# Loading the TensorE-turned part of x ahead of the transposing loads, and copying the padded weights on ScalarE

## The chip, the cores and the metric

One NeuronCore of a Trainium2 chip runs the whole kernel. The metric is device time in microseconds (us) for one execution. The figures of the kernel before are eight timed executions, and one more that the hardware profiler recorded.

## The reference, cut to what matters

```python
x = A_x                                   # 1 x 2048 x 512, bfloat16
g = sigmoid((x * gate_w).sum(-1, keepdims=True))
# A: attention with 32 heads of 16
q, k, v = split_heads(x @ wqkv)
a = softmax(q @ k.T / 4) @ v @ wo
# B: gated feed-forward, hidden width 1792
b = (silu(x @ w_gate) * (x @ w_up)) @ w_down
return g * a + (1 - g) * b
```

The input x enters every product. The attention's exponentials (32 heads, 2048 x 2048 scores each) are most of the work.

## The kernel before, in words

TensorE contracts over partitions, so the products with the weights need x turned: `xT` (line 176) holds x with its 512 columns as four chunks `dc` of 128 partitions, and the 2048 rows along the free axis. The attention works in units of one block of 512 queries and four heads; each unit runs over 16 tiles of 128 keys. For each tile TensorE makes scores (`s_t`, two heads to a tile of 1024 columns), ScalarE takes their exponential (`e_t`), and TensorE multiplies that into `o_ps`. VectorE takes a share of the tiles (`d_t` and `y_t`) by integer arithmetic. Projections, the feed-forward part and the output products are cut in pieces, and a planner with modelled times and due dates (class `Pacer`, lines 48 to 76, and the loop from line 1390) puts these pieces between the score tiles. What comes out is a fixed order of instructions on each engine: `mm`, `act`, `vec` and `queue` (lines 157 to 173) pin that order on TensorE, ScalarE, VectorE and the SyncE (SP) queue.

Before the planner begins there is a prologue, and the change lies wholly in it:

- **Loads.** SP issues six transposing DMAs (line 182), each 1024 rows by 128 columns. For the first half of the rows (0 to 1023) only chunks 0 and 1 come that way; for the second half all four do. I number them T1 to T6 in the order of issue. SP then issues the rest of the value weights (line 194) and of the query and key weights (line 196). ScalarE's queue issues, in this order, 64 columns of the key weights and of the query weights (`wqk`, line 186), the plain load `x_rows` (line 189: rows 0 to 1023, columns 256 to 511, 512 KB, parked in the first part of `wd_t`), and 64 columns of the value weights (line 192).
- **Memsets and padded weights.** VectorE clears small tiles, and twice (lines 239 to 243) sets a group of `kaug` to ones and then copies 64 columns of weights from `wqk` into the spaced layout `wpad`, the key weights first (i = 1), then the query weights (i = 0). `wpad` lies in `mt`.
- **Keeping TensorE busy.** `keep_warm(11)` at line 1026 runs eleven products of a cleared tile into a scratch bank, `warm`.
- **Turning on TensorE.** `turn` (line 1021) multiplies the eight 128 x 128 blocks of a chunk of `x_rows` by an identity: chunk 3 first, which ScalarE copies from `tp` to `xT` (line 1029), then chunk 2, which VectorE copies (line 1033).
- **The first keys and queries.** Lines 1036 to 1043 accumulate `kp0` (1024 keys, two products for each chunk) and `qp0` (512 queries, one product) over the chunks in the order 0, 2, 3, 1, with one more `keep_warm(1)` before the first chunk and between chunks. Chunks 0 and 1 come from T1 and T2, chunks 2 and 3 from `turn`. After that a maximum of the keys (`largest`), a bound, the first values (`v0`), and the first score tile follow, each waiting for the one before.

The planner's first side work is `k0_pieces(2)` and `k0_pieces(3)` (line 1070): keys of the second half, which need T3 to T6. Value pieces (`v_pieces`, line 491) then need the value weights of line 194.

Of the kernel before, what the change touches and what calls it, by code (L numbers as in the profile page):

```python
# [8 lines left out]
ACT = mybir.ActivationFunctionType  # L9
# [70 lines left out]
def kernel(  # L80
# [12 lines left out]
    nc = tc.nc  # L93
    P = 128
    x = A_x.flatten_outer_dims()
    S, D = x.shape
    F = B_w_gate.shape[1]
    DH = 16
# [6 lines left out]
    QBW = 512  # L105
# [40 lines left out]
    def ordered(ins):  # L146
        i = ins.ins
        if i.engine in last_of:
            tc.add_manual_dep(
                i, last_of[i.engine].name,  # L150
                mybir.DependencyInfo(mybir.DependencyClass.NoSync, mybir.DependencyReason.DATA),
                reason="order",
            )
        last_of[i.engine] = i
        return ins

    def mm(*args, **kw):
        return ordered(nc.tensor.matmul(*args, **kw))  # L158

    def act(*args, **kw):  # L160
        ordered(nc.scalar.activation(*args, **kw))  # L161
# [11 lines left out]
    queue = Ordered(nc.sync)  # L173
# [3 lines left out]
    wd_t = big.tile([P, FC, D], BF16, name="wd_t")  # L177
    HALF = DC // 2
    x_rows = wd_t[:, 0:4, :].rearrange("p f d -> p (f d)").rearrange("p (i d) -> p i d", d=HALF * P)
    for t0 in (0, 2 * QBW):  # L180
        for dc in range(DC if t0 else HALF):
            queue.dma_start_transpose(out=xT[:, dc, t0:t0 + 2 * QBW], in_=x[t0:t0 + 2 * QBW, dc * P:(dc + 1) * P])
    wqk = big.tile([P, DC, 2 * D], BF16, name="wqk")
    for c0 in (D, 0):

        nc.scalar.dma_start(out=wqk[:, :, c0:c0 + 64],
                            in_=A_wqkv[:, c0:c0 + 64].rearrange("(dc p) c -> p dc c", p=P))

    nc.scalar.dma_start(out=x_rows, in_=x[0:2 * QBW, HALF * P:D].rearrange("(i p) d -> p i d", p=P))
    rb = big.tile([P, NB, QBW], BF16, name="rb")  # L190
    wv = rb[:, :, :]
    nc.scalar.dma_start(out=wv[:, :, 0:64], in_=A_wqkv[:, 2 * D:2 * D + 64].rearrange("(dc p) c -> p dc c", p=P))
# [2 lines left out]
    for c0 in (D, 0):  # L195
        queue.dma_start(out=wqk[:, :, c0 + 64:c0 + D],
                          in_=A_wqkv[:, c0 + 64:c0 + D].rearrange("(dc p) c -> p dc c", p=P))
# [22 lines left out]
    wpad = [mt[:, i, :].rearrange("p (dc c) -> p dc c", c=P) for i in range(2)]  # L220
# [15 lines left out]
    def ones_rows(engine, g):  # L236

        engine.memset(kaug[:, g, :].bitcast(F32), 1.0019378662109375)
    for i in (1, 0):
        ones_rows(nc.vector, 2 - i)  # L240
        nc.vector.tensor_copy(
            out=wpad[i][:, :, :].rearrange("p dc (j c) -> p dc j c", c=32)[:, :, :, 1:1 + DH],
            in_=wqk[:, :, i * D:i * D + 64].rearrange("p dc (j c) -> p dc j c", c=DH))
    ident = const.tile([P, P], BF16, name="ident")
    nc.gpsimd.memset(ident[:], 1.0)
    nc.gpsimd.affine_select(out=ident[:], in_=ident[:], pattern=[[-1, P]], compare_op=ALU.is_equal,
# [13 lines left out]
    for h in range(8):  # L260
        c = 2 * (h % 4) + h // 4
# [410 lines left out]
    def down_pieces(qb, tq):  # L672

        def end(p):
            t, n = tq, qb * TQ + tq
            share = omg if qb < QB - 1 else ge
            vec.tensor_scalar(out=bblk[:, t, :], in0=p[:, 0:D], scalar1=share[:, n:n + 1],
                              scalar2=None, op0=ALU.mult)
            if qb == QB - 1:
                scaled.add(t)  # L680
            m_free(p, plan.dve)
        return columns(FC, "dps", lambda fc: mt[:, fc, tq * P:(tq + 1) * P], lambda fc: wd_t[:, fc, :],
                       lambda p: later(0.65, lambda: end(p)))
# [314 lines left out]
    def keep_warm(n):  # L998
        for _ in range(n):
            mm(warm[:, :], lhsT=idle[:, 0:P], rhs=idle[:, :], start=True, stop=True)  # L1000
# [22 lines left out]
            mm(ps[k // TQ][:, k % TQ * P:(k % TQ + 1) * P], lhsT=x_rows[:, k, (dc - HALF) * P:(dc - HALF + 1) * P],  # L1023
               rhs=ident[:, :], start=True, stop=True)

    keep_warm(11)
    tp = ps_s.tile([P, 2 * QBW], F32, tag="s", name="tp")
    turn(DC - 1, [tp[:, 0:QBW], tp[:, QBW:2 * QBW]])
    act(out=xT[:, DC - 1, 0:2 * QBW], in_=tp[:, :], func=ACT.Copy)
# [97 lines left out]
    for qb in range(1, QB):  # L1127
        d = qb * KT
# [5 lines left out]
    for qb in range(QB):  # L1134
        for b in range(NB):
            d = UNIT.index((qb, max(2 * b, 1))) * KT
# [30 lines left out]
    for qb in range(QB):  # L1167
# [18 lines left out]
        for tq in range(TQ):  # L1186
            c = pace.add(down_pieces(qb, tq), 0 if qb else 100, a0 + per * (0.6 + 0.3 * (tq + 1) / TQ if qb < QB - 1 else 0.68 + 0.32 * (tq + 1) / TQ), (gus if tq == 0 else prev) + fin_prev + gates)
# [116 lines left out]
    def side(most):  # L1304

        due = any(not c.out() for n in range(plan.slot, plan.slot + 12) for c in need.get(n, []))
        cur = pace.cur
        begun = cur is not None and not cur.out() and cur.i and pace.credit > -3
        c = pick() if pace.credit > 0 or due or begun else None
        if c is None:  # L1310
            return None
        mms, _, takes = c.pieces[c.i][:3]
        mode, two = c.pieces[c.i][3:] or ("C", None)
        if two and two["seq"] == plan.seq:
            return None
        t = m_ready(int(takes)) if takes else 0.0
        if t is None or t > plan.pe or 0.226 * mms + (0.1 if plan.mode != mode else 0.0) > most:
            return None
        return c
# [70 lines left out]
    while au < UNITS:  # L1390
# [10 lines left out]
        if room > 0.02:  # L1401
# [6 lines left out]
            c = side(room + SLACK)  # L1408
# [29 lines left out]
    while closed < UNITS or vops or added or vcur:  # L1438
# [9 lines left out]
        c = side(2.0)  # L1448
# [78 lines left out]
```

## Time and profile before

| | before |
|---|---|
| median of 8 timed executions | 836.04 us (833.89 to 836.71) |
| the profiled execution's own time | 833.6 us |
| span of the profile, first to last instruction | 831.9 us |
| PE (TensorE) busy | 787.5 us (95%), 8117 instructions |
| DVE (VectorE) busy | 796.8 us (96%), 1177 instructions |
| ACT (ScalarE) busy | 810.0 us (97%), 909 instructions |
| POOL (GpSimd) busy | 102.6 us (12%), 124 instructions |
| first exponential of a score tile begins | 17.70 us |
| last score matmul begins | 821.22 us |

The span is the stretch between the first and the last instruction; the execution's own time is 1.7 us more. In the timeline a row has its start, its busy time, the engine, the source line, the operation, the tile written and the tiles read, and in brackets how long the engine stood idle before it and what released it. "ACTq" and "SPq" are those engines' issue of a DMA, not the transfer. In the table by stretches each row has the stretch, its length, the busy time of PE, PEld (weight loads), DVE, ACT and POOL with the number of instructions, the granted TensorE clock as a share of full speed, the busy share of the DMA engines, and GB/s.

### The profile page before, as it was taken

The numbers are of one execution on the slowest core, as the hardware profiler recorded it, in microseconds if no ns is written. First come the engines' busy times: TensorE is split into PE (matmuls) and PEld (weight loads), VectorE is DVE, ScalarE is ACT, GpSimd is POOL, SyncE is SP. The second block draws the span as 40 slices with busy tenths as digits, with TensorE's granted clock in tenths as the row PEclk, the third lists the DMA queues.
The fourth block names the chain that finished last, engine by engine and source line by source line (L and its number), as shares of the span: only waits on it lengthen the run. The fifth ranks groups of instructions, "written<-read, shape, count | busy, mean of one in ns | idle before, by whom it ended". The sixth has DMA issues, their size and how long they took to land.

```text
span 831.9 us, 20393 instructions
## 1 busy us (share of the span) xinstructions
PE 787.5 (95%) x8117; PEld 234.1 (28%) x8118; DVE 796.8 (96%) x1177; ACT 810.0 (97%) x909; POOL 102.6 (12%) x124
## 2 busy tenths in 40 slices
PE   7999999999999999999999999999998989999996
PEld 3322232322222222222222222222222222222222
DVE  5899999999999999999999999999999999999994
ACT  3999999999999999999999999999999999999996
POOL 5010111010101100101111110111111101111100
PEclk9999999999999999999999999999999999999999
DMA  8024347565454345564344464544425455453323
GB/s 177 2 52 97 67 81 138 110 155 100 105 116 84 76 96 112 106 130 88 81 84 87 90 137 88 123 88 100 80 59 115 91 115 107 102 100 72 75 61 76
DMA packets 100647, 79.54 MB, mean 96 GB/s; under 512 B 75696, under 2 KB 88584, under 8 KB 100552
## 3 DMA queue, kind: packets, MB, share of 16 engines
q0 software_dynamic: 12960, 47.19, 29.9%
q1 hardware_dynamic: 84680, 30.07, 15.4%
q10 hardware_dynamic: 2912, 0.98, 0.6%
q8 instruction: 63, 1.03, 0.5%
q14 instruction: 32, 0.26, 0.1%
HBM read 21.36 MB, written 2.34 MB: 28 GB/s over the span
## 4 chain that ended last, share of the span: by engine, by line
PE 38%; ACT 35%; DVE 16%; issue 8%; DMA 2%; SPq 0%; ACTq 0%; DVEq 0%
ACT e_t L161 33%; PE s_t L158 13%; PE o_ps L158 7%; DVE y_t L170 6%; PE gu L158 5%; PE d_t L158 4%; DVE kaug L170 3%; PE dps L158 3%; DVE u_t L170 2%; ACT th L161 2%; PE kp L158 2%; DVE mt L170 2%; PE qp L158 1%; DVE z_t L170 1%; PE vp L158 1%
## 5 line engine op out<-in xcount | busy, mean ns | idle before, releaser
L161 ACT ACTIVATE e_t<-s_t 128x1024 bf16<-128x1024 f32 x844 | 788.1, 1108 | 1.7 <-PE s_t L158 1.2
L158 PE MATMUL s_t<-qx,kaug 64*128 64x512 bf16 x1336 | 273.4, 383 | 25.5 <-ACT e_t L161 22.1
L170 DVE TENSOR_SCALAR y_t<-d_t 128x512 uint16<-128x512 f32 x360 | 234.1, 680 | 1.3 <-PE d_t L158 1.1
L158 PEld LDWEIGHTS <-kaug 64*128 64x128 bf16 x2048 | 112.6, 93 | 341.2 <-issue 332.1
L158 PE MATMUL o_ps<-e_t,vaug 128*32 128x512 bf16 x1688 | 168.1, 390 | 0.3 <-DVE osb L170 0.3
L158 PE MATMUL d_t<-qx,kaug 64*128 64x512 bf16 x296 | 102.1, 380 | 1.4 <-DVE y_t L170 0.6
L791 POOL DMA_DIRECT2D y_t<-u_t x45 | 44.5, 989 | 361.0 <-PE s_t L158 167.4
L158 PEld LDWEIGHTS <-vaug 128*32 128x32 bf16 (+1 forms) x2060 | 50.6, 93 | 120.8 <-issue 119.8
L158 PE MATMUL gu<-xT,wg 128*32 128x512 bf16 x896 | 76.8, 383 | 0.3 <-DMA wg<-in_B_w_gate_dram 0.3
L158 PE MATMUL dps<-wd_t,mt 128*32 128x512 bf16 x896 | 76.1, 383 | 0.0
L791 POOL DMA_DIRECT2D y_t<-kaug x39 | 40.5, 1039 | 284.2 <-PE s_t L158 120.3
L158 PE MATMUL gu<-xT,wu 128*32 128x512 bf16 x896 | 73.4, 382 | 0.1
L170 DVE TENSOR_SCALAR y_t<-y_t 128x2048 uint16<-128x2048 uint16 x90 | 61.4, 682 | 5.6 <-DMA y_t<-u_t 4.0
L170 DVE TENSOR_SCALAR z_t<-y_t 128x2048 uint16<-128x2048 uint16 x90 | 61.7, 686 | 1.0
L170 DVE TENSOR_TENSOR u_t<-u_t 128x2048 f16<-128x2048 f16 x45 | 54.9, 1221 | 0.9
L170 DVE TENSOR_TENSOR u_t<-u_t,z_t 128x2048 f16<-128x2048 f16 x45 | 54.6, 1213 | 0.1
L170 DVE TENSOR_TENSOR kaug<-kaug 128x2048 f16<-128x2048 f16 x39 | 47.6, 1221 | 0.9
L158 PE MATMUL s_t<-q,kaug 64*128 64x512 bf16 x212 | 43.2, 382 | 5.2 <-ACT e_t L161 4.6
L170 DVE TENSOR_TENSOR kaug<-kaug,z_t 128x2048 f16<-128x2048 f16 x39 | 47.4, 1215 | 0.1
L170 DVE SCALAR_TENSOR_TENSOR mt<-gs,gu 128x512 bf16<-128x512 bf16 x56 | 38.2, 682 | 2.6 <-PE gu L158 0.2
L161 ACT ACTIVATE th<-gu 128x512 bf16<-128x512 f32 x56 | 38.5, 688 | 0.0
L170 DVE SCALAR_TENSOR_TENSOR gs<-th,gu 128x512 bf16<-128x512 bf16 x56 | 37.9, 676 | 0.2 <-ACT th L161 0.2
(133 smaller groups left out, 561.9 us busy)
## 6 DMA issues: line engine op xcount, KB each, us to landing
y_t<-u_t POOLq DMA_DIRECT2D x45, 512.0 KB, 4.9
y_t<-kaug POOLq DMA_DIRECT2D x39, 512.0 KB, 5.0
wg<-in_B_w_gate_dram SPq DMA_DIRECT2D x56, 128.0 KB
wu<-in_B_w_up_dram SPq DMA_DIRECT2D x56, 128.0 KB
y_t<-wd_t POOLq DMA_DIRECT2D x6, 512.0 KB, 4.6
on<-osb SPq DMA_DIRECT2D x120, 16.0 KB
rb<-rr SPq DMA_DIRECT2D x15, 128.0 KB
wd_t<-in_B_w_down_dram SPq DMA_DIRECT2D x7, 256.0 KB
```

The lines of the kernel that those rows point to most:

```text
L158: return ordered(nc.tensor.matmul(*args, **kw))
L161: ordered(nc.scalar.activation(*args, **kw))
L170: return lambda *a, **kw: ordered(f(*a, **kw))
L791: nc.gpsimd.dma_start(out=ya, in_=ua, accum_op=ALU.add)
```

## The change

Three edits in the prologue. The plain load `x_rows` moves from third place on ScalarE's queue to first place on SP's, ahead of the six transposing loads. The two copies into `wpad` move from VectorE to ScalarE, and VectorE keeps the two memsets between which they stood. The opening `keep_warm` has eight products in place of eleven. On every engine the order of the other instructions is unchanged.

```diff
     x_rows = wd_t[:, 0:4, :].rearrange("p f d -> p (f d)").rearrange("p (i d) -> p i d", d=HALF * P)
+    queue.dma_start(out=x_rows, in_=x[0:2 * QBW, HALF * P:D].rearrange("(i p) d -> p i d", p=P))
     for t0 in (0, 2 * QBW):
         for dc in range(DC if t0 else HALF):
             queue.dma_start_transpose(out=xT[:, dc, t0:t0 + 2 * QBW], in_=x[t0:t0 + 2 * QBW, dc * P:(dc + 1) * P])
...
-    nc.scalar.dma_start(out=x_rows, in_=x[0:2 * QBW, HALF * P:D].rearrange("(i p) d -> p i d", p=P))
     rb = big.tile([P, NB, QBW], BF16, name="rb")
...
     for i in (1, 0):
+        act(out=wpad[i][:, :, :].rearrange("p dc (j c) -> p dc j c", c=32)[:, :, :, 1:1 + DH],
+            in_=wqk[:, :, i * D:i * D + 64].rearrange("p dc (j c) -> p dc j c", c=DH), func=ACT.Copy)
         ones_rows(nc.vector, 2 - i)
-        nc.vector.tensor_copy(
-            out=wpad[i][:, :, :].rearrange("p dc (j c) -> p dc j c", c=32)[:, :, :, 1:1 + DH],
-            in_=wqk[:, :, i * D:i * D + 64].rearrange("p dc (j c) -> p dc j c", c=DH))
...
-    keep_warm(11)
+    keep_warm(8)
```

## The prediction

> **What bounds the kernel now.** The page comes first. Three engines are busy nearly all the time, so the steady part has no slack. The change touches only what stands before it.
>
> ```profile
> PE 787.5 (95%) x8117; PEld 234.1 (28%) x8118; DVE 796.8 (96%) x1177; ACT 810.0 (97%) x909; POOL 102.6 (12%) x124
> ```
>
> From the first exponential at 17.70 us on, ScalarE hardly rests. Every order on an engine is fixed and nothing later is tied to an absolute time, so what the prologue saves should reach the end one for one, if no load is late. The timeline shows what the prologue waits for.
>
> ```profile
> 1.84 0.53 ACTq L189 DMA_DIRECT2D wd_t<-in_A_x_dram  x1
> ...
> 8.24 1.07 PE L158 MATMUL tp<-ident,wd_t 128*128 128x128 bf16 x16 [2.12 <-DMA wd_t<-in_A_x_dram]
> ...
> 13.21 0.38 PE L158 MATMUL qp<-xT,mt 128*128 128x512 bf16 x1
> 13.43 0.38 PE L158 MATMUL warm<-mt 128*128 128x512 bf16 x1
> 13.64 0.59 PE L158 MATMUL kp<-xT,mt 128*128 128x512 bf16 x2
> 14.07 0.38 PE L158 MATMUL qp<-xT,mt 128*128 128x512 bf16 x1
> ...
> 14.27 1.23 DVE L170 TENSOR_REDUCE kpart<-kp 128x1 f32<-128x1024 f32 x1 [3.86 <-PE kp L158]
> ```
>
> The eleven warm-up products end near 6.12; TensorE then stands 2.12 us for `x_rows`, 6.40 us after its issue. From 8.24 everything up to the maximum `kpart` is one chain on TensorE, ending at 14.29 (the next group, `vp`, begins there): 6.05 us. The table by stretches shows that this chain is also slow (third last column: granted clock).
>
> ```profile
> 2.57:5.98 3.41, 3.41 (x9) 1.00 (x7) 3.03 (x8) 1.28 (x1) 3.41 (x5) 1.00 1.26 215
> 5.98:9.40 3.42, 1.30 (x19) 1.04 (x19) 0.84 (x4) 0.50 (x1) 3.03 (x10) 1.00 1.29 198
> 9.40:12.81 3.41, 3.41 (x10) 1.17 (x9) 1.01 (x2) 0.53 (x1) 2.80 (x4) 0.50 1.06 211
> 12.81:16.22 3.41, 2.85 (x44) 1.73 (x42) 1.58 (x2) 1.28 (x2) 0.00 (x0) 1.00 1.01 280
> 16.22:19.64 3.42, 2.22 (x30) 0.82 (x26) 2.92 (x4) 2.85 (x4) 0.00 (x0) 1.00 0.44 147
> ...
> 825.18:828.59 3.41, 1.68 (x25) 0.76 (x23) 2.46 (x7) 0.82 (x2) 0.00 (x0) 1.00 0.00 0
> ```
>
> The stretches are cut where the clock changes. After one with PE busy 1.30 of 3.42 us (38%) the clock is 0.50 for 3.41 us. After 2.22 (65%) it stays full. The stretch from 825.18 had 1.68 (49%), and 0.50 follows it too. So in this trace the dividing share lies between 49% and 65%. The wait for `x_rows` therefore costs twice: 2.12 us of standing, and 3.41 us of the following chain at half speed.
>
> **The load (edit 1).** Its issue moves from 1.84 to about 0.81, where SP now begins with T1, a gain of 1.03 us. It also no longer has T1's packets in front of it. In the DMA view, queue q1 (SP) moved 1013 packets, 0.26 MB (T1), between 2.4 and 4.0 us, while q10 (ScalarE) moved 480; only from 4.0 to 7.6 did q10 move 1408 packets with `x_rows` in them. PE started 0.64 us after that (8.24). In the new order SP's first packets should start near 2.25 (11 packets of q1 fell before 2.4), 1.44 us after the issue. For the transfer I have two ends. Between 5.0 and 6.2 us q10 moved 563 packets; at that rate 1024 packets take 2.2 us. The slow end is the 3.6 us of its own row, shared there with T2 and the value weights. In the new place it shares with the 1024 small packets of `wqk` instead, which is less, so I take 3.0. Landing: 2.25 + 3.0 + 0.64 = 5.9 us, with ends 5.1 and 6.5. Against 8.24 that is 2.3 earlier.
>
> **Transposes moved behind.** SP's queue is moved past by one issue (0.53 us by the old ScalarE row) and 0.5 MB. T1 now follows `x_rows`: packets 5.25 to 6.4 or 6.95 (1152 packets of q1 went in the 1.0 us from 9.0; T1 itself took 1.6 to 1.7), then 0.64, so it is there between 7.0 and 7.6. PE wants it for the first `kp` at 5.9 + 1.07 (`tp`) + 0.22 (`warm`) = 7.2. I charge the upper end, 0.4; below, nothing. T2 needs 1.0 us more of packets and shares with the value weights, about 8.3 to 9.3; it is wanted last, at 10.2 or later. T3 to T6 are behind by no more than the DMA engines lose by the new order, since the bytes are the same; in the old trace q1's packets of 256 B gave way to larger ones by 13.3. `k0_pieces(2)` started at 18.26 and moves to about 14.9, and wants T6 only with its last chunk, near 15.8. The value weights of line 194 are a third of the 1.34 MB that q1 moved from 13.3 to 18.1, so they are there by about 15.5, and the first `v_pieces` product moves from 21.51 to about 18.1: covered. If T6 came 1 us later than now, the cover still holds; beyond 2 us each further us costs one, because the piece stands in PE's queue ahead of score tiles.
>
> **The clock and eight warm-up products (edit 3).** The old eleven took 4.86 us, 0.42 to 0.44 each; eight end near 1.26 + 8 x 0.424 = 4.65. Up to 5.9 PE then stands 1.25 us. On the grid of this trace the stretch 2.57 to 5.98 would have 2.08 + 0.08 = 2.16 us of work, 63%, next to the 65% after which the clock stayed full. The next stretch is solid work. Then the chain runs at full speed: 1.07 for the sixteen turns, 0.22 for `warm`, three rounds at 0.87 (13.21 to 14.07 shows one at full speed: `qp`, `warm`, `kp` twice) and a last round of 0.66, together 4.56 against 6.05. That is 1.5 us.
>
> The Trainium skill, page "TensorE: Matmul & The Clock Gate", section "What's actually happening", gives the reason in its own terms: half speed is the default, and it is lifted only after a busy window of about 3.4 us of a grid that runs free of the kernel's start. The steps of 3.41 us here agree; that the grid's place differs from run to run no view of one execution can show. By that rule three warm-up products fewer are a risk; if it bit, the 1.5 us would be lost and the sum would be 2.3 - 0.4 = 1.9.
>
> **The copies on ScalarE (edit 2).** VectorE's two took 1.38 and 2.45 us (from 4.01 on) and ended near 6.54; nothing waited for them, since PE came to `kp` at 9.36. Left there they would still have been done before 7.2, so their removal counts nothing. On ScalarE no such row exists: its row for 512 columns is 0.59 us, for 1024 columns 1.02, so I take 0.4 each, with ends of 0 and 0.6. They follow the table load (3.04 to 4.32; 0.5 earlier without the issue of `x_rows`) and wait for `wqk`, whose packets ended before 4.4 in the old trace and may now end near 5. So they run between 4 and 6.2. Queued behind them is the copy of `tp`, which can begin about 6.6 and is needed by the third round at 8.9 less its own 1.02. The cover is 1.3 us; every us beyond would be added.
>
> A second place in the skill speaks against edit 1: "DMA: Bandwidth & Descriptors", section "Issuing engines are not separate DMA queues", says that transfers from all engines interleave on the same DMA engines and that choosing another issuer saves only the issue time. By it alone the landing would move by the 1.03 us of issue and no more. The order of packets above (T1 ahead, then `x_rows`) weighs against so small a gain.
>
> **The sum.** 2.3 (landing) + 1.5 (clock) - 0.4 (T1) = 3.4 us. On the profiled execution: 833.6 - 3.4 = 830.2. The timed runs have a median of 836.04, 2.4 above it, and spread over 2.8 us; the stretch 14.29 to 17.70 with 1.89 us of PE work (55%) lies between the two shares, so a differently placed grid may add a half-speed step both before and after. I carry the difference over to the median: 836.04 - 3.4 = **832.6 us**.
>
> **Rivals.**
> - *The clock drops anyway.* If `x_rows` lands near 6.5 or the dividing share is at 64%, PE's gap leads to the same half-speed step. For it: 63% is at the margin, and the old gap of 2.12 us did it. Against: a later grid has more work in it. Gain 1.7 to 1.9 less up to 0.4, about 1.6: 834.4. Chance 0.15.
> - *The change doesn't bring the load forward.* The DMA engines are the limit (the DMA share is above 1 from 2.57 to 9.40), the small packets of `wqk` and slow stretches (175 packets of q10 between 4.4 and 5.0) fall into its time. Landing 7.5 to 8.2, gain 0 to 0.7: 835.6. Against it: T1's bytes are no longer in front. Chance 0.08.
> - *Slower: the clock falls ahead of the turn and twice.* Place: PE between 4.65 and the landing. If the load comes later than about 7.5, eight products leave a gap of 3 us; then the turn runs at half speed too (+1.07) and the sparse stretch after it (55%) brings another half-speed step of 3.41 us (+1.7), less what was gained (0.3 to 0.7): about +2.2, 838.2. It needs a landing hardly earlier than now. Chance 0.08.
>
> **How the numbers follow.** Forecast 0.69, rivals 0.15, 0.08 and 0.08. About 0.2%, 1.67 us, is what a measurement here can tell from no change: faster means below 834.37. The forecast and more than half of the first rival lie there: 0.78; within: 0.14; slower: 0.08. Range: the early landing (5.1) adds 0.8 and T1's 0.4 may fall away: 836.04 - 4.6 = 831.4. At the top it takes in the first rival and 0.4 for T1: 834.8.
>
> **What would show it.** Right: `tp` begins between 5.1 and 6.5, the granted clock is 1.00 from there to 14 us, `kpart` begins near 10.9, the first exponential near 14.3, and `k0_pieces(2)` follows without a wait. Wrong: a clock of 0.50 in the `kp` rounds; `kp` waiting for `xT` by DMA; the copy of `tp` standing behind the copies of `wpad`; or `tp` still beginning after 7 us.

## The result, and the profile after

The changed kernel takes 831.87 us (median of 12 runs, 830.33 to 833.06) against 835.63 us (34 runs, 833.89 to 837.96). The ratio is 0.9955, with a 95% interval of 0.9948 to 0.9963: 3.8 us faster, 3.4 forecast.

The two profiled executions do not show that by themselves. The one after took 833.06 us, the slowest of its twelve; the one before took 833.6, less than any of its eight timed ones. This is the timeline of the one after, PE and ACT:

```profile
5.51 1.28 ACT L161 ACT_TABLE_LOAD   x1 [5.51 <-DMA wqk<-in_A_wqkv_dram]
...
5.79 1.07 PE L158 MATMUL tp<-ident,wd_t 128*128 128x128 bf16 x16 [1.11 <-DMA wd_t<-in_A_x_dram]
...
6.80 0.92 ACT L161 ACTIVATE mt<-wqk 128x256 bf16<-128x256 bf16 x2
...
7.93 1.01 PE L158 MATMUL kp<-xT,mt 128*128 128x512 bf16 x2 [0.85 <-DMA xT<-in_A_x_dram]
...
10.44 0.63 PE L158 MATMUL qp<-xT,mt 128*128 128x512 bf16 x1
...
12.75 1.23 DVE L170 TENSOR_REDUCE kpart<-kp 128x1 f32<-128x1024 f32 x1 [4.79 <-PE kp L158]
```

The turn begins at 5.79 instead of 8.24. But the first `kp` then waits 0.85 us for T1, and the products of the next rounds take 0.63 us again. `kpart` starts 1.52 us earlier than before, not 3.4. The table by stretches, cut at this execution's clock steps (PE busy is the third number, the granted clock the third from the end):

```profile
0.96:4.38 3.42, 3.12 (x8) 1.04 (x8) 2.58 (x20) 0.00 (x0) 3.38 (x15) 1.00 0.65 159
4.38:7.79 3.41, 1.58 (x19) 1.05 (x18) 1.93 (x3) 2.23 (x4) 3.02 (x13) 1.00 1.34 197
7.79:11.20 3.41, 3.27 (x8) 1.13 (x8) 0.17 (x1) 0.82 (x1) 3.41 (x4) 0.50 1.23 231
```

In this execution the grid lay so that both gaps, 1.11 us ahead of the turn and 0.85 ahead of `kp`, fell into one stretch (46% busy), and the half-speed step came after all: the first rival's picture. Of the prediction's four signs of being wrong, three stand in this execution: the clock of 0.50 in the `kp` rounds, `kp` waiting for `xT` by DMA, and ScalarE's copy of `tp` (at 7.61) behind its copies of `wpad`. Later VectorE waited 1.34 us for an accumulating DMA (until 143.15); a little behind that, by the 143rd exponential, the lead had fallen from 1.5 to 0.6 us. So whether the clock term is real can't be read from this pair; the experiments have to tell it by medians.

### The profile page after: what moved, and what is told of

Same layout as the page of the kernel before. It is cut to its first block, busy times and chain, and to the rows that moved or that the text cites. A ratio compares the mean times of both kernels' runs of the same rounds, so it can differ in the third digit from the quotient of the medians.

```text
span 831.3 us, 20388 instructions
## 1 busy us (share of the span) xinstructions
PE 785.9 (95%) x8114; PEld 233.8 (28%) x8115; DVE 795.2 (96%) x1175; ACT 810.9 (98%) x911; POOL 102.2 (12%) x124
## 3 DMA queue, kind: packets, MB, share of 16 engines
q8 instruction: 63, 1.03, 0.5%
## 4 chain that ended last, share of the span: by engine, by line
PE 30%; ACT 27%; DVE 17%; issue 7%; DMA 3%; SPq 0%; DVEq 0%; ACTq 0%; POOLq 0%
ACT e_t L161 25%; PE s_t L158 10%; PE o_ps L158 6%; DVE y_t L170 6%; PE gu L158 5%; PE d_t L158 4%; DVE u_t L170 3%; DVE kaug L170 3%; PE dps L158 2%; ACT th L161 2%; DVE mt L170 1%; DVE z_t L170 1%; DMA y_t<-wd_t 1%; PE a_ps L158 1%; DMA y_t<-u_t 1%
```

## The experiments

**One part alone, one part out, and the clock alone.**

e1_load_only is the kernel before with the change's first edit alone:

```diff
+    queue.dma_start(out=x_rows, in_=x[0:2 * QBW, HALF * P:D].rearrange("(i p) d -> p i d", p=P))
     for t0 in (0, 2 * QBW):
...
-    nc.scalar.dma_start(out=x_rows, in_=x[0:2 * QBW, HALF * P:D].rearrange("(i p) d -> p i d", p=P))
```

e2_load_copies_warm11 is the changed kernel with the old number of products:

```diff
-    keep_warm(8)
+    keep_warm(11)
```

e3_load_warm8 is the changed kernel with the copies as before:

```diff
-        act(out=wpad[i][:, :, :].rearrange("p dc (j c) -> p dc j c", c=32)[:, :, :, 1:1 + DH],
-            in_=wqk[:, :, i * D:i * D + 64].rearrange("p dc (j c) -> p dc j c", c=DH), func=ACT.Copy)
         ones_rows(nc.vector, 2 - i)
+        nc.vector.tensor_copy(
+            out=wpad[i][:, :, :].rearrange("p dc (j c) -> p dc j c", c=32)[:, :, :, 1:1 + DH],
+            in_=wqk[:, :, i * D:i * D + 64].rearrange("p dc (j c) -> p dc j c", c=DH))
```

e4_before_warm19 is the kernel before with more products:

```diff
-    keep_warm(11)
+    keep_warm(19)
```

> The kernel before with the plain load moved to the front of SP's queue, and nothing else (copies into wpad on VectorE, eleven warm-up products). Theory as predicted (the load and the clock carry the gain, the copies count nothing): the turn begins near 5.9, time 832 to 832.5, within 0.5 of the changed kernel's 831.9. Rival (the copies matter): in the changed kernel's profile the key weights had landed only at 5.51 and the query weights later, so VectorE's two copies of 1.4 to 2.4 us would begin no sooner than that, with the copies of tp queued behind them; the first qp would then wait until about 9.5, 1 to 2 us later than with copies on ScalarE: 833 to 834.

> The changed kernel with eleven warm-up products in place of eight. Theory: eleven end at 5.92 or 6.1, with the load there at 5.8, so the gap of 1.1 us closes at a cost of at most 0.3, and the clock falls in fewer executions: 831.0 to 832.0. Rival (fewer products are a gain of their own, because the turn stands behind them): 832.2 or more.

> The changed kernel with the two copies into wpad put back on VectorE. Theory as predicted (the copies count nothing): 831.9. Rival (the copies matter once the load is in front): the first kp and qp wait for VectorE, 833 to 834, and the granted clock falls for longer because TensorE stands in the meantime.

> The kernel before with nineteen warm-up products in place of eleven, so that TensorE works until the load lands at 8.2, and nothing else. Theory (the half-speed step after the gap costs about 1.5 us of the chain): granted clock 1.00 from 6 to 14 us, turn still at 8.2, 1.5 less, 834.1. Rival (the clock is not what the time hangs on): 835.6 as before. Second rival (the products get in the way of the turn): above 835.6.

Measured, beside 835.37 for the kernel before: the load alone 831.60 (ratio 0.9954, interval 0.9938 to 0.9969), the change with eleven products 831.44 (0.9951, 0.9932 to 0.9969), the change with the copies on VectorE 831.68 (0.9953, 0.9938 to 0.9967), the kernel before with nineteen products 833.31 (0.9967, 0.9952 to 0.9982). The load carries the change; the copies and the three fewer products can't be told from nothing. Eight more products ahead of the turn, with no load moved, gain 2.1 us. But they did not last until the load was there, as they were meant to: in the profiled execution of e4 they came 0.22 us apart from 4.27 on, in place of 0.43, the last ended at 7.01, and TensorE then stood as long as in the kernel before:

```profile
9.16 1.07 PE L158 MATMUL tp<-ident,wd_t 128*128 128x128 bf16 x16 [2.16 <-DMA wd_t<-in_A_x_dram]
```

The clock stayed full all the same from there through the rounds: on this grid the stretch with the gap was 57% busy. The load came 0.9 us later than in the kernel before, and the execution, at 834.65, was the slowest of its eight. So the 2.1 us stand on the medians; this profile shows a half-speed step moved from the rounds to a later place, and not a gap that was filled.

The rival of e1, that VectorE's copies would hold up the first `qp`, fell. They did begin only when the weights had landed, at 5.57 and 7.35, but took 0.88 and 0.26 us, not 1.4 to 2.4, and were done when the first `kp` began at 7.91.

e1 also shows where a half-speed step goes when it isn't ahead of `kp`. Table by stretches of e1:

```profile
5.42:8.83 3.41, 2.58 (x24) 1.45 (x23) 2.72 (x5) 1.02 (x1) 3.02 (x11) 1.00 1.33 230
8.83:12.24 3.41, 3.41 (x44) 2.00 (x42) 1.11 (x1) 0.60 (x1) 3.35 (x4) 1.00 1.09 202
12.24:15.66 3.42, 1.65 (x21) 0.70 (x24) 2.63 (x6) 2.69 (x4) 0.00 (x0) 1.00 0.96 262
15.66:19.07 3.41, 3.41 (x32) 0.64 (x28) 3.18 (x7) 1.87 (x2) 0.00 (x0) 0.50 0.51 174
```

The rounds of `kp` ran at full speed here and the first exponential began at 14.57, 3.1 us ahead of the profile before. But the dependent steps after them (maximum, bound, first score tile) leave PE 48% busy, and the next 3.41 us ran at half speed, where PE has score tiles and keys to make. By the 21st exponential 1.6 of the 3.1 us were left. e2, e3 and e4 show the same step.

**The clock held, in both kernels.** If that is the reason, filling all the gaps with products must leave the load's own part.

e5_after_filled is the changed kernel with these edits; e6_before_filled is the kernel before with the same last two lines added, 24 products in the first place, and the single product ahead of the rounds left as it is.

```diff
-    keep_warm(8)
+    keep_warm(11)
...
-    keep_warm(1)
+    keep_warm(4)
     arrived = (0, 2, 3, 1)
...
     v0(0)
+    keep_warm(3)
     bound_add(qp0, kneg1, aq0)
+    keep_warm(4)
```

> The changed kernel with TensorE kept working through every gap of the prologue: 11 warm-up products at the start in place of 8, 4 in place of 1 between the turn and the first kp, and new ones after v0 (3) and before the first score tile (4). Theory (what still separates executions is a half-speed step that falls after a sparse stretch): no granted clock of 0.50 between 6 and 30 us, the first exponential near 14.6 and that lead kept to 40 us; 830.3, 1.5 below the changed kernel. Rival (the clock is no longer worth anything once the load is early): 831.9. Second rival (the products stand in the way): 832.3 or more.

> The kernel before with TensorE kept working the same way: 24 warm-up products at the start in place of 11, 3 after v0 and 4 before the first score tile. Theory: with no half-speed step in either kernel, what is left between this one and the filled changed kernel is the landing of the load less the new wait for T1, 2.45 - 0.85 = 1.6 in the two profiles; so 832.0 to 832.7, below the 833.3 of nineteen products at the start alone. Rival (the clock was the whole effect of the change): within 0.5 of the filled changed kernel.

Measured, beside 835.38: 831.04 (0.9945, 0.9934 to 0.9957) and 833.41 (0.9976, 0.9966 to 0.9986). The five runs of e5 lie within 0.54 us and the nine of e6 within 1.44, those of the changed kernel within 2.7 and of the kernel before within 4.1. Table by stretches of e5:

```profile
2.63:6.05 3.42, 3.42 (x11) 1.14 (x10) 2.02 (x6) 0.60 (x1) 3.42 (x5) 1.00 1.21 253
6.05:9.46 3.41, 3.41 (x29) 2.01 (x28) 1.29 (x2) 2.46 (x4) 3.02 (x11) 1.00 1.31 232
9.46:12.87 3.41, 3.41 (x47) 1.92 (x45) 1.57 (x2) 1.24 (x2) 2.55 (x3) 1.00 1.04 178
12.87:16.29 3.42, 3.15 (x34) 1.08 (x30) 2.92 (x4) 2.82 (x4) 0.00 (x0) 1.00 1.03 337
16.29:19.70 3.41, 3.41 (x44) 0.87 (x42) 3.19 (x8) 3.17 (x5) 0.00 (x0) 1.00 0.19 61
```

No stretch is under 92%, and the clock doesn't fall. By the medians filling is worth 835.38 - 833.41 = 2.0 us to the kernel before, which is clear of noise, and 831.87 - 831.04 = 0.8 to the changed kernel, which is not: 831.04 lies halfway between the theory's 830.3 and the rival's 831.9 (no worth left in the clock), and the two intervals overlap (0.9934 to 0.9957, and 0.9948 to 0.9963). With the clock full in both, the load is worth 833.41 - 831.04 = 2.4 us; that is clear, and the rival of e6, that the clock was the whole effect, fell. (2.37 + 1.97 - 0.83 gives 3.5, the distance of 831.87 from 835.38, whatever the four times are; it confirms nothing.) Both times were above what I expected (830.3, and 832.0 to 832.7). In the two profiles the first exponentials stand at 16.00 and 14.43, 1.57 us apart. First e6, then e5:

```profile
8.18 1.07 PE L158 MATMUL tp<-ident,wd_t 128*128 128x128 bf16 x16 [0.25 <-DMA wd_t<-in_A_x_dram]
9.30 0.59 PE L158 MATMUL kp<-xT,mt 128*128 128x512 bf16 x2
```

```profile
5.93 1.12 PE L158 MATMUL tp<-ident,wd_t 128*128 128x128 bf16 x16
7.75 0.59 PE L158 MATMUL kp<-xT,mt 128*128 128x512 bf16 x2
```

The turn begins 2.25 us earlier, and the first `kp`, which needs T1, comes 1.82 after it in place of 1.12: 2.25 - 0.70 = 1.55. That is the theory's picture, landing less T1, with these executions' own numbers. The other 0.8 us of the 2.4 comes later, in small steps at several places; I have not traced it.

**The queue or the order.**

e7_load_first_on_act puts the load, in the same line of the changed kernel, on ScalarE's queue, where it is then first:

```diff
-    queue.dma_start(out=x_rows, in_=x[0:2 * QBW, HALF * P:D].rearrange("(i p) d -> p i d", p=P))
+    nc.scalar.dma_start(out=x_rows, in_=x[0:2 * QBW, HALF * P:D].rearrange("(i p) d -> p i d", p=P))
```

e8_t1_then_load keeps it on SP's queue, behind T1:

```diff
-    queue.dma_start(out=x_rows, in_=x[0:2 * QBW, HALF * P:D].rearrange("(i p) d -> p i d", p=P))
     for t0 in (0, 2 * QBW):
         for dc in range(DC if t0 else HALF):
             queue.dma_start_transpose(out=xT[:, dc, t0:t0 + 2 * QBW], in_=x[t0:t0 + 2 * QBW, dc * P:(dc + 1) * P])
+            if t0 == dc == 0:
+                queue.dma_start(out=x_rows, in_=x[0:2 * QBW, HALF * P:D].rearrange("(i p) d -> p i d", p=P))
```

> The changed kernel with the plain load first on ScalarE's queue, ahead of the two small weight loads, in place of first on SP's. Theory (what counts is its place in the order of issue, not the queue): turn begins between 5.6 and 6.2, T1 is issued at 0.8 and lands no later than 7.9, time 831.4 to 832.2. Rival (the queue counts: T1 issued at the same moment on SP takes the DMA engines first): turn after 7, time 833 to 835.

> The changed kernel with the plain load on SP's queue behind the first transposing load T1 and ahead of the other five. Theory (T1's place in front is what held the load back): T1 lands near 5.2 and the load between 7.0 and 8.2, so at most half of the gain is left: 833.0 to 834.5. Rival (being ahead of T2 to T6 and of ScalarE's small loads is what counts): 831.5 to 832.3.

Measured, beside 835.38: 831.34 (0.9955, 0.9937 to 0.9972) and 834.17 (0.9981, 0.9972 to 0.9991). From ScalarE's queue, first in place, the turn began at 5.45; behind T1 on SP's queue it began at 7.44 (first e7, then e8):

```profile
5.45 1.07 PE L158 MATMUL tp<-ident,wd_t 128*128 128x128 bf16 x16 [0.77 <-POOL sbc_t L265]
```

```profile
7.44 1.07 PE L158 MATMUL tp<-ident,wd_t 128*128 128x128 bf16 x16 [2.59 <-DMA wd_t<-in_A_x_dram]
```

Between these two queues, the place in the order counts for the landing and the queue doesn't. e7 pays elsewhere for its early turn: the weights on the same queue came later, and `kp` waited 2.08 us for ScalarE's copy into `wpad`. In that execution (833.41, the second slowest of six, which run from 830.16 to 834.15) the first exponential came at 18.33, later than in the kernel before; so e7's gain is shown by its median alone. In e8 the longer gap ahead of the turn also brought a half-speed step over the rounds, so its loss is not the landing alone.

**What is left of the change without the load.**

e11_copies_warm8_only is the kernel before with the edit of the copies (the diff of e3, the other way) and:

```diff
-    keep_warm(11)
+    keep_warm(8)
```

> The changed kernel with the plain load put back on ScalarE's queue in third place: only the copies on ScalarE and eight warm-up products are left of the change. Theory (the load carries all of it): no gain; the gap ahead of the turn grows from 2.1 to about 3.5 us and the clock falls as often or earlier: 835.4 to 836.6. Rival (copies or fewer products give a part of their own): below 834.9.

Measured: 834.68 beside 835.43 (0.9992, 0.9983 to 1.0001). The median is on the rival's side of the line (834.9) by 0.2 us, but the interval takes in no change, so this stays undecided. In its profile the turn itself runs at half speed, 1.89 us instead of 1.07, after a stretch in which PE did nothing, and a second half-speed step begins at 18.56. That is the picture of the slower rival, and yet the median isn't slower. The kernel before gains 2.0 us on the median when its gaps are filled, so it may lose as much to such steps; this was not told apart.

**Towards a better version.**

e10_load_filled is e5 with the copies back on VectorE (the diff of e3). e9_load_filled_chunk3_first differs from e10 in this:

```diff
-    keep_warm(4)
-    arrived = (0, 2, 3, 1)
+    keep_warm(3)
+    arrived = (3, 0, 2, 1)
```

e12_chunk3_first_later is e9 with five products there in place of three.

> Looking for a better version: the load in front, copies on VectorE, the gaps filled as in the filled changed kernel, and the first kp rounds taken in the chunk order 3, 0, 2, 1, so that the first round doesn't wait for T1 but for ScalarE's copy of tp, which ended at 7.48 when only the load was moved. Theory (the wait for T1, 0.8 us, is now the late one): the first kp at 7.5 in place of 7.75 to 7.9, 0.3 to 0.4 below the same kernel in the old chunk order, 830.6. Rival (T2 or the VectorE copies of chunk 2 are late next): no gain, 831.0.

> The filled changed kernel with the copies into wpad back on VectorE. Theory (the copies have 0.3 us or more to spare on either engine): 831.0, spread under 1 us. Rival (with the clock steady, the engine of the copies shows): 0.4 or more away from 831.04.

> The best version so far (load in front, gaps filled, chunk 3 first, 829.17) with two more warm-up products ahead of the first kp, so that its prologue ends 0.4 us later, 0.15 after that of the same kernel in the old chunk order (830.40). In the two profiles the prologues differ by 0.28 us, the medians by 1.23; the rest, 0.9, arises near 126 us, where VectorE waits 1.48 us for an accumulating DMA in the one and 0.21 in the other. Theory (chunk order only moves the prologue; whether that DMA is late depends on how things meet in time): about 830.5. Rival (the new chunk order itself takes that wait away): 829.6.

Measured: e9 829.17 and e10 830.40, beside 835.43 (0.9926, 0.9914 to 0.9939, and 0.9940, 0.9926 to 0.9953). e9 beats both kernels, by 2.7 us the changed one. In its timeline no round waits for T1:

```profile
5.81 1.06 PE L158 MATMUL tp<-ident,wd_t 128*128 128x128 bf16 x16
6.71 0.81 PE L158 MATMUL warm<-mt 128*128 128x512 bf16 x3
7.54 0.59 PE L158 MATMUL kp<-xT,mt 128*128 128x512 bf16 x2
```

Its first exponential is at 14.22, that of e10 at 14.50. That explains 0.28 us of the 1.23 between their medians. In the profiles the rest arises where VectorE waits for an accumulating DMA near 125 us. First e10, then e9, timeline of VectorE:

```profile
125.31 0.69 DVE L170 TENSOR_SCALAR y_t<-y_t 128x2048 uint16<-128x2048 uint16 x1 [1.48 <-DMA y_t<-wd_t]
```

```profile
123.76 0.69 DVE L170 TENSOR_SCALAR y_t<-y_t 128x2048 uint16<-128x2048 uint16 x1 [0.21 <-DMA y_t<-wd_t]
```

e12 was to tell whether the new chunk order itself takes that wait away. In its profile the wait is back (1.2 us), and the lag behind e9 grows from 0.35 to 0.95 us over the 121st and 122nd exponential, which speaks for a meeting in time. Its median, 830.18, lies between the two expectations, and it ran on a chip where the kernel before took 836.52, so its ratio (0.9927, 0.9913 to 0.9940) is e9's. What decides when that DMA is late stays open. e10 at 830.40 is 0.64 us from e5, on the side that its rival had named for the engine of the copies (0.4 or more); but the two ran beside different runs of the kernel before, their intervals overlap (0.9926 to 0.9953, and 0.9934 to 0.9957), and their first exponentials stand at 14.50 and 14.43. It is not decided.

## Why the prediction was right, point by point

- **Landing, 5.9 (5.1 to 6.5).** Right, 5.79, by errors that cancel. The packets of `x_rows` began at 1.94 in place of 2.25 and took 2.9 us in place of 3.0; the turn began 0.94 us after the last one, not 0.64.
- **T1, charged 0.4 (there by 7.0 to 7.6).** Under-sized: 0.85 us, `kp` at 7.93. It was not the packets. In the DMA view (queue, packets, MB, share) of the changed kernel from 0 to 6.08 us, SP's queue had moved 1024 of `x_rows`, 1024 of T1 and 16 of 4 bytes:

```profile
q1 hardware_dynamic: 2064, 0.79, 57.6%
```

  So T1's packets were over by 6.08, ahead of my 6.4 to 6.95 (the early end should have been 6.1 by the rate beside it), although ScalarE's weights were moving at the same time, from 4.8 to 6.6:

```profile
q1 hardware_dynamic: 1100, 0.27, 85.6%
q10 hardware_dynamic: 1056, 0.13, 48.5%
```

  What I had wrong is the time from the last packet to the landing: I took 0.64 from the plain load, and for T1 it was 1.86 (6.07 to 7.93). The kernel before had it in its trace: T1's packets ended at 3.99 there, and its semaphore was full at 5.37, 1.38 later. Why it takes longer for this load is open. The other 0.1 us is that TensorE came to `kp` at 7.08 and not at 7.2.
- **Clock, 1.5.** The size of one step was right: from the first `kp` to `kpart` took 4.82 us in the changed kernel's profile, with the half-speed step, and 3.22 in e1's, without. Its place was too simple. I took one half-speed step out at one place; in these profiles each execution without filled gaps has such steps where its grid meets a stretch with too little work: over the turn (e11), over the rounds, or after them. I had named the place after the rounds but not priced it. By medians filling says 2.0 - 0.8 = 1.2 of my 1.5, and the 0.8 in it is not clear of noise. The load's part is 2.4 where I had 2.3 - 0.4 = 1.9; that the two errors nearly cancel in the sum is luck.
- **63% of work, next to the 65% that held the clock.** This argument for eight products was wrong, and no run tested it. The column says 1.00 from the start, but the trace's clock record begins only with the first step, at 5.98 in the kernel before. Up to there a product took as long as in the rounds at 0.50. All products ahead of the turn in the kernel before (shortest, median and longest, ns), then e4's from 4.7 us on, behind its first step at 4.27:

```profile
L158 PE MATMUL warm<-mt x11: 608/634/634, 1.3 to 5.5; 128*128 128x512 bf16 x11
```

```profile
L158 PE MATMUL warm<-mt x11: 379/379/379, 4.5 to 6.6; 128*128 128x512 bf16 x11
```

  So TensorE begins at half speed, and a stretch with 63% would have had to raise the clock, not to hold it. In e7 a stretch with 70% did not. In the profiles with eight products the stretch ahead of the first step was at least 81% busy, by the place of the grid and not by my sum.
- **"On the profiled execution: 830.2".** Wrong: 833.06. In that execution the clock term was not gained at all, T1 cost 0.45 more, and another us of lead went where the late accumulating DMA stands. `kpart` began at 12.75 and the first exponential at 16.19, not at 10.9 and 14.3. Only the median follows the sum.
- **Copies, nothing.** Right in the time (e3), wrong in a step: I had `wqk` there near 5 and the table load at 2.5 to 3.8. The key weights landed at 5.51, and ScalarE's table load, behind a wait for them, ran from 5.51 to 6.79. The copy of `tp` began at 7.61 in place of 6.6, so 1.0 of the 1.3 us of cover was used up, and PE, late itself, came to the third round only at 11.25.
- **Eight products, a risk.** Eleven are no worse: 831.44 against 831.87 for eight, inside the intervals. In e2's profile the turn follows the products without a gap.
- **The two rules of the skill.** "DMA: Bandwidth & Descriptors" says the issuing engine saves only issue time. e7 agrees on the engine (831.34 against 831.87); the 2.45 us earlier turn, where issue moved by 1.03, shows that the order of issue is another matter. "TensorE: Matmul & The Clock Gate" has the grid running free of the kernel: its steps, counted from the first instruction, stood at 5.98, 4.38, 5.42 and 6.05 in four of these executions, which agrees. The page lets the clock fall after an idle window; here 46% to 51% of work was too little to hold it, and the measurement decides.

## What to carry to other kernels

A wait ahead of TensorE work can cost twice, once by itself and once in the half-speed step after it; price both, and look at every sparse stretch nearby, since a step taken out at one place can come back at the next. Take the time from a load's last packet to its landing from a load of the same kind. Where a prologue is a chain, products that nobody reads are a cheap thing to try: with no load moved, 2.1 us of e1's 3.8 for one line; on top of the moved load, 0.8 at most, inside the noise. It also made runs alike: the five versions with filled gaps (e5, e6, e9, e10, e12) spread over 0.5 to 1.4 us in five to nine runs, all others over 2.0 to 6.2 in six or more. Compare medians of several executions before reading one profile against another: the two profiles of this case differ by 0.5 us, the medians by 3.8.

## What the runs showed of the hardware that was not expected

- **The clock falls and rises at different shares.** At full speed it fell after stretches with PE busy 46% (the changed kernel) to 51% (1.73 of 3.41 us in e3), and after emptier ones, and stayed after 56% (1.91 in e7) and 57% (1.93 in e4). At half speed, 70% did not lift it in e7, while 81% (2.75) did in e3, where the record begins with that step at 5.50 and the column ahead of it says 1.00. First e7, then e3:

```profile
4.37:7.78 3.41, 1.58 (x19) 0.95 (x17) 2.10 (x3) 0.76 (x1) 3.02 (x13) 1.00 1.34 217
7.78:11.19 3.41, 2.38 (x6) 0.88 (x7) 0.00 (x0) 2.16 (x4) 3.41 (x4) 0.50 1.24 222
11.19:14.61 3.42, 3.42 (x9) 1.21 (x8) 0.00 (x0) 0.00 (x0) 0.80 (x1) 0.50 0.93 217
14.61:18.02 3.41, 1.91 (x40) 1.36 (x38) 2.50 (x4) 2.20 (x3) 0.00 (x0) 1.00 0.81 276
```

```profile
2.09:5.50 3.41, 2.75 (x7) 0.72 (x5) 1.44 (x10) 1.28 (x1) 3.41 (x8) 1.00 0.98 212
12.33:15.74 3.41, 1.73 (x20) 0.72 (x24) 2.62 (x6) 2.77 (x4) 0.00 (x0) 1.00 0.89 218
145.45:148.86 3.41, 2.25 (x24) 1.08 (x21) 3.31 (x6) 3.16 (x4) 0.00 (x0) 1.00 0.06 14
148.86:152.27 3.41, 3.41 (x23) 0.69 (x24) 3.33 (x6) 2.17 (x4) 0.99 (x1) 0.50 0.13 29
```

  One case doesn't fit: in e3, after VectorE had waited 1.2 us for an accumulating DMA (until 142.67), the clock fell after a stretch with 66% (2.25 of 3.41), though the kernel before held it after 65%. Half of the lead of 1.8 us was gone by the 143rd exponential, which began 0.5 us into the half-speed step, and all of it by the 145th. So the share of busy PE, as this profile counts it, doesn't decide alone; what else does was not tried.
- **A small transfer can wait behind a large one of another queue.** `wqk`'s first 64 KB were issued at 0.80 in both kernels, 0.01 us before SP's first DMA. In the kernel before they led, and ScalarE's queue had moved 528 packets by 3.0 us; in the changed kernel it had moved none by then. It is `x_rows` alone that the DMA view of the changed kernel shows from 1.8 to 3.0:

```profile
q1 hardware_dynamic: 269, 0.14, 48.8%
```

  The issue of `wqk` ended at 1.29 there, that of `x_rows` at 1.26; in the kernel before they ended at 1.25 (`wqk`) and 2.09 (T1). The load whose issue ended first went first; whether that is the reason was not tried.
- **The same VectorE copy took 0.26 to 2.45 us.** The two copies of 128 x 256 elements took 2.45 and 1.38 in the kernel before, where their records overlap (4.01 to 6.55 together), and 0.88 and 0.26 in e1. What slowed them was not tried.
